# Decode attention with a gated MLP on one core: all eight sets inside PE's loop, and the last weight rows as 512-column products

## The chip, the cores and the metric

The kernel runs on one core of a Trainium2 chip. The time is device time in microseconds for one execution; several executions are timed and their median is given. One execution is also recorded by the hardware profiler, and all rows below come from that one. In them PE is the matrix engine (PEld its weight loads), DVE the vector engine, ACT the scalar engine, POOL GpSimd, SP the engine whose queue issues the large loads.

## What is computed

Four sequences, one new token each. From `x` (4 x 512):

```python
x = A_x
g = _sigmoid((x * gate_w).sum(-1, keepdims=True))
a = _A_ref(x, A_k_cache, A_v_cache, A_wq, A_wo)   # 32 query heads, 8 kv heads, head size 128, last 4096 cached rows
b = _B_ref(x, B_W_gate, B_W_up, B_W_down)         # relu(x Wg) * (x Wu), then times Wd; inner width 1792
return g * a + (1 - g) * b
```

`a` is `softmax(q k^T / sqrt(128)) v` over the window, with four query heads to a kv head, then times `wo` (4096 x 512). The caches are bf16, and the window of both is 67 MB, out of 81 MB that the kernel loads. The output is 4 x 512.

## The kernel before

**Sets.** The work on the caches is cut into eight sets. A set is one sequence and four kv heads: K of a set is 4 MB (`Ksb[:, s % 2]`), V is 4 MB (`Vsb[:, s % 2]`), both double buffered. For a set s PE turns K over in 16 fills of four transposes each (`kt(s, i)`, L363, four PSUM banks `TR` in turn); ACT copies 11 of the fills back over K (L368) and DVE five (L370). After every four fills `scores(s, bank)` multiplies with the queries `qS` (eight products of 512 columns in four column groups of 32, L384, banks `SCB[0]` and `SCB[1]` in turn), and DVE masks the result into `sc` with a running maximum (L392). One set later follow, for s - 1: `maximum` (DVE over the banks' maxima, a PE product that spreads it, DVE to `negmax`; L398 to L403), `exponent` on ACT in two pieces (L411), `turn` on DVE (transposes to `pT`, L418), `values` on PE (64 products with V in four column groups into bank `OB`, L429) and a copy to `osb` (L435). Two sets later `combine` sums the groups on PE (L443, L447) and DVE scales into `oq` (L450, L451).

**Order.** Every engine has a list of operations, written out by hand in one order for all engines; `Program.need` turns each operation's waits (named events) into semaphore counts. PE alone runs part of its list as a loop: `turn_edge` marks places in the list, and `emit` checks that the turns between the marks have the same waits and emits one of them in a hardware loop, lowering the semaphores at the end of a turn by what a turn raises (L138 to L145). PE's list is: the queries and the gate; set 0's fills and scores by themselves; set 1; then three turns of two sets each (2 and 3, 4 and 5, 6 and 7); then the end. Where PE waits for an event that DVE counts on its other semaphore, `need` takes the next event on the semaphore that PE reads.

**Loads.** All large loads are in SP's queue, in this order: Wq (to `Wbig`), K0, K1, V0, K2, V1, K3, V2, and so on to K7, V6, then Wg, Wu, V7, Wd, and `wo` in five pieces (rows 0 to 15, 16 to 25, 26 to 29 of 32, and rows 30 and 31 in two halves; `WO_CUTS`). K of set s waits for `("SC", s - 2, 3)`, the last scores of the set that held its buffer; V of set s waits for `("PV", s - 2, 3)`, the last values product there; both from set 2 on. Wd waits for `("PV", 6, 3)`, and `wo`, which takes Wq's place in `Wbig`, for the query products. Each load runs on 16 DMA engines, and its semaphore is raised by each of them when its sixteenth is in place: 16 landing marks to a load.

**Start.** POOL makes identity, mask and selection matrices and clears `xw`, `xT` and `qW` (L252 to L284). `x` and `gate_w` come by ACT's queue. DVE spreads x (`XW`, L290), PE transposes it, DVE copies it to `gwB` and `xT` (L298, L301), PE and ACT make the gate; PE multiplies with Wq (32 products of 512 columns in four column groups, L314), ACT casts (L324), PE transposes the heads (L332), DVE and ACT each write half of `qW` (L338), POOL copies a set's part to `qS` (L343).

**End.** After the loop: `maximum`, `exponent` and `turn` of set 7, `combine(6)`, `gateup` (Wg and Wu, L459), values of set 7 when V7 has landed, `combine(7)`, then the two output products. They add up in one bank, `AB = SCB[0]`, four column groups of 128 output columns each: for each of Wd's 14 rows of 128 and `wo`'s 32, four products of 128 columns (`product`, L530), so 56 and 128 of them. `wo`'s wait piece by piece for their load. DVE and ACT then copy two groups each (L548, L550) and SP stores.

Of the kernel before, what the change touches and what calls it, by code (L numbers as in the profile page):

```python
# [19 lines left out]
NSET = 8  # L20
# [6 lines left out]
NTR = 4  # L27
# [4 lines left out]
WO_CUTS = (0, 16, 26, 30)  # L32
ACT_TAKES = (0, 1, 4, 6, 8, 9, 11, 12, 13, 14, 15)
LOOP_FIRST = 2
LOOP_TURNS = 3


class Program:

# [8 lines left out]
    def __init__(self):  # L48
        self.ops = {e: [] for e in self.ENGINES}
        self.events = {}  # L50
        self.counts = {}
        self.history = {}
        self.dmas = []
        self.turns = []
        self.shared = {}

    def op(self, engine, fn, name=None, waits=(), sem=None):
        if name is not None:
            assert name not in self.events, name
            sem = sem or engine  # L60
            self.counts[sem] = self.counts.get(sem, 0) + 1
            self.events[name] = (sem, self.counts[sem], engine, len(self.ops[engine]))
            self.history.setdefault(sem, []).append(len(self.ops[engine]))
        self.ops[engine].append((fn, name, tuple(waits), False))

# [12 lines left out]
    def need(self, engine, waits):  # L78
        need = {}
        for w in waits:  # L80
            if w is None:
                continue
            s, n, by, at = self.events[w]
            for own, mine in (("dve", "vd"), ("act", "va")):
                want = mine if engine == "pe" else own
                if by == own and s in (own, mine) and s != want:
                    s = want
                    n = 1 + sum(1 for k in self.history[s] if k < at)
                    assert n <= self.counts[s], w
            need[s] = max(need.get(s, 0), n)  # L90
        return need
# [5 lines left out]
    def emit_list(self, eng, sems, engine, ops, shift, seen):  # L97
        for fn, name, waits, is_dma in ops:
# [5 lines left out]
            if fn is None:  # L104
                continue
# [17 lines left out]
    def emit(self, engine, eng, sems):  # L123
# [6 lines left out]
        first = self.signature(ops[t[0]:t[1]], {})  # L130
        for k in range(1, len(t) - 1):
            shift = {s: k * n for s, n in self.lowered.items() if s not in self.shared}
            assert self.signature(ops[t[k]:t[k + 1]], shift) == first, k
        with eng.Fori(0, len(t) - 1):
            self.emit_list(eng, sems, engine, ops[t[0]:t[1]], {}, {})
# [3 lines left out]
        shift = {s: (len(t) - 1) * n for s, n in self.lowered.items() if s not in self.shared}  # L139
        self.emit_list(eng, sems, engine, ops[t[-1]:], shift, {})  # L140


def bass_gated_mix__sliding_block_cached__glu_gated_reglu__decode_kernel(
# [13 lines left out]
    with ExitStack() as ctx:  # L157
# [7 lines left out]
        pT = sb("pT", [128, 2, 2048], BF16)  # L165
# [11 lines left out]
        xT = sb("xT", [128, 4, 32], BF16)  # L177
        xw = sb("xw", [5, 512], FP32)
        gwB = sb("gwB", [128, 512], BF16)
        gsb = sb("gsb", [128, 8], FP32)  # L180
        qW = sb("qW", [128, NSET, 2, 32], BF16)
        qS = sb("qS", [128, 2, 2, 32], BF16)
        mx = sb("mx", [128, 2, NBANK], FP32)
        mcol = sb("mcol", [128, 2], FP32)
# [3 lines left out]
        rowsum = sb("rowsum", [128, 2, NPIECE], FP32)  # L188
        osb = sb("osb", [128, 2, 256], FP32)
# [5 lines left out]
        hT = sb("hT", [128, NFT * 4], BF16)  # L195
        outr = sb("outr", [4, 512], BF16)
        banks = [ctx.enter_context(nc.psum_tensor("bank%d" % i, [128, 512], FP32)) for i in range(8)]
# [9 lines left out]
        Wq3 = Wbig[:, :].rearrange("p (t w) -> p t w", t=4)  # L207
# [4 lines left out]
        def loop_sem(kind, s):  # L212
            if kind == "K" and s >= LOOP_FIRST or kind == "V" and LOOP_FIRST - 1 <= s < NSET - 1:
                return "%s%d" % (kind, s % 2)
            return None
# [9 lines left out]
        def load_v(s):  # L225
            P.dma("sp", lambda e: e.dma_start(Vsb[:, s % 2, :], heads(A_v_cache, s)), ("V", s),
                  [("PV", s - 2, 3)] if s >= 2 else [], sem=loop_sem("V", s))
# [15 lines left out]
        for k in range(len(WO_CUTS) - 1):  # L243
            lo, hi = 512 * WO_CUTS[k], 512 * WO_CUTS[k + 1]
            P.dma("sp", lambda e, lo=lo, hi=hi: e.dma_start(Wbig[:, lo:hi], wo_src[:, lo:hi]), ("WO", k), [("Q",)])
        wo_src3 = A_wo.rearrange("(p i) w -> p i w", p=128)
        for u in range(2):
            P.dma("sp", lambda e, u=u: e.dma_start(Wo3[:, WO_CUTS[-1]:32, 256 * u:256 * u + 256],
                                                   wo_src3[:, WO_CUTS[-1]:32, 256 * u:256 * u + 256]), ("WOL", u), [("Q",)])
# [8 lines left out]
        P.op("pool", lambda e: e.memset(xw[:, :], 0.0), ("XW0",))  # L258
        P.op("pool", lambda e: e.memset(xT[:, :, :].rearrange("p t r -> p (t r)"), 0.0))
        P.op("pool", lambda e: e.memset(qW[:, :, :, :].rearrange("p s h w -> p (s h w)"), 0.0), ("QZ",))  # L260
# [34 lines left out]
        for t in range(4):  # L295
            P.op("pe", lambda e, t=t: e.transpose(FB[:, t * 8:t * 8 + 5], xv[0:5, t, :], identw[0:5, 0:5]),  # L296
                 ("XT",) if t == 3 else None, [("XW",), ("IDENTW",)])
        P.op("dve", lambda e: e.tensor_copy(gwB[:, :].rearrange("p (t m) -> p t m", t=4),  # L298
                                            fx[:, :, 4:5].to_broadcast([128, 4, 128])),
             None, [("XT",)])  # L300
        P.op("dve", lambda e: e.tensor_copy(xT[:, :, 0:4], fx[:, :, 0:4]), ("XTC",), [("XT",), ("QZ",)], sem="vd")  # L301
        for t in range(4):
            P.op("pe", lambda e, t=t: e.matmul(FB[:, 32:36], gwB[:, t * 128:(t + 1) * 128], xT[:, t, 0:4],
                                               start=(t == 0), stop=(t == 3)),
                 ("Z",) if t == 3 else None, [("XTC",)])
# [31 lines left out]
        for cc in range(2):  # L337
            P.op(("dve", "act")[cc], lambda e, cc=cc: (e.copy if cc else e.tensor_copy)(  # L338
                qW[64 * cc:64 * cc + 64, :, :, 16 * cc:16 * cc + 16].rearrange("p s o j -> p (s o) j"),
                FB[64 * cc:64 * cc + 64, 64:320].rearrange("p (k j) -> p k j", j=16)),  # L340
                ("QC", cc), [("QT",), ("QZ",)])
# [5 lines left out]
        fills = []  # L347

        def copy_done(f):
            return ("KTC",) + fills[f]  # L350

        def kt(s, i):
            f = len(fills)
            fills.append((s, i))
            bk = TR[f % NTR]
            for cc in range(4):
                c = 4 * i + cc
                w = []
                if cc == 0:
                    w = [("K", s), ("IDENTW",)] + ([copy_done(f - NTR)] if f >= NTR else [])  # L360
                    if i == NTR - 1 and s >= 1:
                        w.append(("NEGMAX", s - 1))
# [9 lines left out]
        def scores(s, bank):  # L372
# [4 lines left out]
            for o in range(2):  # L377
                for a in range(4):
                    w = []
                    if a == 0 and o == 0:  # L380
                        w = [("KTC", s, 4 * bank + u) for u in range(4)] + [("QS", s)]
                        if prev >= 0:
                            w.append(("SCC", prev // NBANK, prev % NBANK))
# [12 lines left out]
        def maximum(s):  # L396
            par = s % 2
            P.op("dve", lambda e: e.tensor_reduce(mcol[:, par:par + 1], mx[:, par, :], AXIS.X, ALU.max),  # L398
                 ("MCOL", s), [("SCC", s, NBANK - 1), ("MT", s - 2) if s >= 2 else None], sem="vd")
            P.op("pe", lambda e: e.matmul(TR[NTR - 1][:, 0:128], mcol[:, par:par + 1].to_broadcast([128, 128]), identw[:, :],  # L400
                                          start=True, stop=True),
                 ("MT", s), [("MCOL", s), ("KTC", s, NFILL - 1)])
            P.op("dve", lambda e: e.tensor_tensor_reduce(  # L403
                mrow[:, :], TR[NTR - 1][:, 0:128], qmask[:, :], -SCALE, -LOWEST, ALU.add, ALU.min, negmax[:, par:par + 1]),
# [4 lines left out]
        def exponent(s, k):  # L409
            par = s % 2  # L410
            P.op("act", lambda e: e.activation(  # L411
                sc[:, par, k * PW:(k + 1) * PW], sc[:, par, k * PW:(k + 1) * PW], ACTF.Exp,
                bias=negmax[:, par:par + 1], scale=SCALE, accum_out=rowsum[:, par, k:k + 1]),
                ("EXP", s, k), [("NEGMAX", s), ("SUMS", s - 2) if s >= 2 else None])

        def turn(s, k):
            par = s % 2
            P.op("dve", lambda e: e.transpose(pT[:, par, k * PW:(k + 1) * PW], sc[:, par, k * PW:(k + 1) * PW]),  # L418
                 ("PTT", s, k), [("EXP", s, k), ("PV", s - 2, 3) if s >= 2 else None], sem="vd")

        def values(s, k):
            par = s % 2
            for c in range(16):
                g = c % 4
                w = []
                if c == 0:
                    w = [("PTT", s, k * NPIECE // 4), ("V", s), ("OSB", s - 1) if s >= 1 else None]
# [6 lines left out]
            if k == 3:  # L434
                P.op("act", lambda e: e.copy(osb[:, par, :], OB[:, 0:256]), ("OSB", s),  # L435
                     [("PV", s, 3), ("SUMS", s - 2) if s >= 2 else None], sem="va")

        def combine(s):
            par, b, half = s % 2, s // 2, s % 2
            r = slice(64 * half, 64 * half + 64)  # L440
            for k in range(8):
# [3 lines left out]
                     [("OSB", s), ("WSUM",), ("OQ", s - 1) if s >= 1 else None])  # L445
            for k in range(NPIECE):
                P.op("pe", lambda e, k=k: e.matmul(FB[r, 416:417], Wsum[:, :], rowsum[:, par, k:k + 1],  # L447
                                                   start=(k == 0), stop=(k == NPIECE - 1)),
                     ("SUMS", s) if k == NPIECE - 1 else None, [])
            P.op("dve", lambda e: e.reciprocal(recip[r, par:par + 1], FB[r, 416:417]), ("RECIP", s), [("SUMS", s)])  # L450
# [4 lines left out]
        def gateup():  # L455
            for which, W, key in ((0, Wg, "WG"), (1, Wu, "WU")):
                for t in range(4):
                    for g in range(4):
# [4 lines left out]
                            [(key,)] + [copy_done(f) for f in range(NSET * NFILL - NTR, NSET * NFILL)])  # L463
# [7 lines left out]
                hT[:, :].rearrange("p (i b) -> p i b", b=4),  # L471
# [5 lines left out]
        for i in range(NFILL):  # L477
            kt(0, i)
            if i % 4 == 3 and i > 3:
                scores(0, i // 4 - 1)  # L480
        scores(0, 3)
        for s in range(1, NSET):
            if s >= LOOP_FIRST and (s - LOOP_FIRST) % 2 == 0:
# [12 lines left out]
            if s >= 2:  # L496
                combine(s - 2)
# [35 lines left out]
        for i in range(NFT):  # L533
            for cb in range(4):
                product(hT[:, 4 * i:4 * i + 4], Wd[:, i, :], cb, i == 0, False, None,
                        [("WD",), ("H",), ("SCC", NSET - 1, NBANK - 1)])
        for k in range(len(WO_CUTS) - 1):
            for i in range(WO_CUTS[k], WO_CUTS[k + 1]):
                for cb in range(4):
                    product(oq3[:, :, i], Wo3[:, i, :], cb, False, False, None, [("WO", k), ("OQ", NSET - 1)])  # L540
# [12 lines left out]
        per = {}  # L553
        for s in ("vd", "va"):
            eng = {"vd": "dve", "va": "act"}[s]
            a = P.events[("KTC", LOOP_FIRST, next(i for i in range(NFILL) if (i in ACT_TAKES) == (s == "va")))][1]
            b = P.events[("KTC", LOOP_FIRST + 2, next(i for i in range(NFILL) if (i in ACT_TAKES) == (s == "va")))][1]
            per[s] = b - a
        per["pq"] = 2
# [3 lines left out]
        P.lowered = per  # L563

# [3 lines left out]
        nc.sync.dma_start(Wbig[:, :], A_wq.rearrange("(p t) w -> p (t w)", p=128)).then_inc(sems["wq"], 16)  # L568
# [51 lines left out]
```

## Time and profile before

| | us |
|---|---|
| median of three runs | 196.4 (196.17 to 196.47) |
| the profiled execution | 196.17 |
| its span, first to last instruction | 194.9 |
| PE, DVE, ACT, POOL busy | 139.4, 77.2, 76.1, 9.5 |
| mean granted PE clock | 0.889 |
| K and V, issue to landing, median | 21.8 and 30.9 |

The span is cut into 40 slices in the page's second part; a digit is the busy share of a slice in tenths. The clock is the share of full speed that PE was granted; in this trace it is 1.0 or 0.5. The chain of waits starts at the last instruction and goes back, at each step to what released it. In a group row, "line engine operation out<-in" is followed by shapes, count, busy time, mean duration and the idle time before it. In the timeline a row is start, duration, engine, line, operation, count.

### The profile page before, as it was taken

The page shows a single profiled execution, that of the slowest core. Times are in us where ns is not written, and L with a number is a line of the kernel's source. Part 1 is how long each engine was busy: PE and PEld are TensorE (multiplying, and loading weights), DVE is VectorE, ACT ScalarE, POOL GpSimd, SP SyncE. Part 2 cuts the span into 40 slices and gives each one's busy share as a digit, 9 for nine tenths or more (in the row PEclk, how much of TensorE's full clock was granted, in tenths as well). Part 3 has the DMA queues.
Part 4 walks back from the last instruction along what each step waited for, and adds up shares of the span by engine and source line. Part 5 has one row for each costly group of instructions (what it writes and reads, how often), then busy time and mean ns, then how long its engine had stood idle before and what let it go on. Part 6 is the DMA issues. An engine that isn't in the chain of part 4 may idle for free.

```text
span 194.9 us, 3931 instructions
## 1 busy us (share of the span) xinstructions
PE 139.4 (72%) x1728; PEld 103.6 (53%) x1728; DVE 77.2 (40%) x169; ACT 76.1 (39%) x140; POOL 9.5 (5%) x41
## 2 busy tenths in 40 slices
PE   0135399688789818996898189995995899643834
PEld 0112397366468517763685177854773777422633
DVE  0100045477268302762583026623952456280101
ACT  2005136494285404462854043445641545240001
POOL 8700000000000000000000000000000000000000
PEclk9999999999999995899999855799999579995855
DMA  6999999999999999999999999999999999998993
GB/s 216 444 437 430 430 444 434 430 430 430 440 430 417 437 427 430 437 437 427 430 430 444 430 437 430 430 430 430 430 430 430 430 386 427 479 430 381 429 397 102
DMA packets 3884, 81.16 MB, mean 416 GB/s; under 512 B 409, under 2 KB 930, under 8 KB 1058
## 3 DMA queue, kind: packets, MB, share of 16 engines
q1 hardware_dynamic: 3864, 81.01, 97.3%
q8 instruction: 8, 0.13, 0.3%
q14 instruction: 2, 0.02, 0.0%
q10 hardware_dynamic: 10, 0.01, 0.0%
HBM read 81.01 MB, written 0.00 MB: 416 GB/s over the span
## 4 chain that ended last, share of the span: by engine, by line
DMA 55%; PE 36%; ACT 4%; DVE 3%; issue 1%; SPq 1%; DVEq 0%
DMA Ksb<-in_A_k_cache_dram 43%; PE bank L363 23%; DMA Wbig<-in_A_wo_dram 11%; PE bank L384 6%; ACT Ksb L368 3%; PE bank L429 2%; PE bank L443 2%; DVE Ksb L370 1%; PE bank L530 1%; ACT L411 1%; ACT sc L411 1%; DVE pT L418 1%; PE bank L447 0%; DVE sc L392 0%; PE bank L400 0%
## 5 line engine op out<-in xcount | busy, mean ns | idle before, releaser
L363 PE MATMUL bank<-identw,Ksb 128*128 128x128 f32 x512 | 77.0, 307 | 20.8 <-DMA Ksb<-in_A_k_cache_dram 14.9
L363 PEld LDWEIGHTS bank<-identw,Ksb 128*128 128x128 f32 x512 | 65.3, 158 | 31.6 <-DMA Ksb<-in_A_k_cache_dram 15.8
L368 ACT COPY Ksb<-bank 128x512 f32<-128x512 f32 x88 | 48.7, 589 | 73.0 <-PE bank L363 73.0
L370 DVE COPY Ksb<-bank 128x512 f32<-128x512 f32 x40 | 27.3, 684 | 40.6 <-PE bank L363 40.6
L392 DVE CUSTOM_DVE_ANT_0 sc<-bank,mask 128x512 bf16<-128x512 f32 x32 | 21.8, 682 | 28.8 <-PE bank L384 28.8
L429 PE MATMUL bank<-Vsb,pT 128*32 128x256 bf16 x512 | 20.9, 291 | 6.1 <-DMA Vsb<-in_A_v_cache_dram 6.1
L384 PE MATMUL bank<-Ksb,qS 128*32 128x512 bf16 x256 | 21.0, 405 | 1.8 <-ACT Ksb L368 0.9
L418 DVE STREAM_TRANSPOSE pT<-sc 128x1024 bf16<-128x1024 bf16 x16 | 19.7, 1236 | 2.1 <-ACT sc L411 2.0
L429 PEld LDWEIGHTS bank<-Vsb,pT 128*32 128x32 bf16 x512 | 13.3, 101 | 12.6 <-issue 8.8
L411 ACT ACTIVATE sc<-sc,negmax 128x1024 bf16<-128x1024 bf16 x16 | 18.4, 1151 | 1.9 <-DVE negmax L403 1.8
L443 PEld LDWEIGHTS bank<-osb,Wsel 128*64 128x64 f32 x128 | 9.4, 157 | 4.8 <-issue 3.7
L443 PE MATMUL bank<-osb,Wsel 128*64 128x32 f32 x128 | 10.3, 239 | 0.5 <-ACT osb L435 0.5
L435 ACT COPY osb<-bank 128x256 f32<-128x256 f32 x8 | 3.0, 373 | 17.6 <-PE bank L429 17.6
L400 PE MATMUL bank<-identw,mcol 128*128 128x128 f32 x16 | 3.8, 320 | 7.8 <-DVE mcol L398 4.7
L384 PEld LDWEIGHTS bank<-Ksb,qS 128*32 128x32 bf16 x256 | 4.1, 95 | 9.0 <-ACT Ksb L368 5.7
L400 PEld LDWEIGHTS bank<-identw,mcol 128*128 128x128 f32 x16 | 2.4, 187 | 10.2 <-DVE mcol L398 8.4
L343 POOL COPY qS<-qW 128x64 bf16<-128x64 bf16 x8 | 1.8, 238 | 120.5 <-PE bank L384 110.8
L530 PE MATMUL bank<-Wbig,oq 128*4 128x128 bf16 x128 | 4.2, 307 | 3.8 <-DMA Wbig<-in_A_wo_dram 3.8
L296 PE MATMUL bank<-identw,xw 5*128 5x5 f32 x4 | 0.6, 263 | 8.6 <-DVE xw L290 8.6
L450 DVE RECIPROCAL recip<-bank 64x1 f32<-64x1 f32 x8 | 1.3, 159 | 11.4 <-PE bank L447 11.4
L530 PEld LDWEIGHTS bank<-Wbig,oq 128*4 128x4 bf16 x128 | 3.1, 118 | 4.8 <-DMA Wbig<-in_A_wo_dram 4.7
L314 PE MATMUL bank<-Wbig,xT 128*32 128x512 bf16 x32 | 3.6, 631 | 2.7 <-DMA Wbig<-in_A_wq_dram 2.7
(55 smaller groups left out, 45.4 us busy)
## 6 DMA issues: line engine op xcount, KB each, us to landing
Ksb<-in_A_k_cache_dram SPq DMA_DIRECT2D x8, 4096.0 KB, 21.8
Vsb<-in_A_v_cache_dram SPq DMA_DIRECT2D x8, 4096.0 KB, 30.9
Wbig<-in_A_wq_dram SPq DMA_DIRECT2D x1, 4096.0 KB, 12.2
Wbig<-in_A_wo_dram SPq DMA_DIRECT2D x1, 2048.0 KB, 19.5
Ksb<-in_B_W_gate_dram SPq DMA_DIRECT2D x1, 1792.0 KB, 17.1
Ksb<-in_B_W_up_dram SPq DMA_DIRECT2D x1, 1792.0 KB, 21.0
Vsb<-in_B_W_down_dram SPq DMA_DIRECT2D x1, 1792.0 KB, 15.0
Wbig<-in_A_wo_dram SPq DMA_DIRECT2D x1, 1280.0 KB, 22.1
```

What stands on the lines that cost most here:

```text
L314: P.op("pe", lambda e, half=half, t=t, g=g, col=col: e.matmul(SCB[half][32 * g:32 * g + 32, 0:512], xT[:, t, :], Wq3[:, t, col:col + 512], ...
L363: P.op("pe", lambda e, bk=bk, cc=cc, c=c, s=s: e.transpose(bk[:, cc * 128:(cc + 1) * 128], Kw[:, s % 2, c * 128:(c + 1) * 128], identw[:, :]),
L368: P.op("act", lambda e: e.copy(dst, bk[:, :]), ("KTC", s, i), [("KT", s, i)], sem="va")
L370: P.op("dve", lambda e: e.tensor_copy(dst, bk[:, :]), ("KTC", s, i), [("KT", s, i)], sem="vd")
L384: P.op("pe", lambda e, a=a, o=o: e.matmul(bk[32 * a:32 * a + 32, 0:512], qS[:, s % 2, o, :], k4[:, 16 * bank:16 * bank + 16, 32 * a:32 * a ...
L392: P.op("dve", lambda e: e.tensor_tensor_reduce(sc[:, s % 2, bank * 512:(bank + 1) * 512], bk[:, :], mask[:, :], 1.0, LOWEST, ALU.add, ALU.max,
L400: P.op("pe", lambda e: e.matmul(TR[NTR - 1][:, 0:128], mcol[:, par:par + 1].to_broadcast([128, 128]), identw[:, :], start=True, stop=True) ...
L411: P.op("act", lambda e: e.activation(sc[:, par, k * PW:(k + 1) * PW], sc[:, par, k * PW:(k + 1) * PW], ACTF.Exp, bias=negmax[:, par:par + ...
L418: P.op("dve", lambda e: e.transpose(pT[:, par, k * PW:(k + 1) * PW], sc[:, par, k * PW:(k + 1) * PW]), ("PTT", s, k), [("EXP", s, k), ("PV ...
L429: P.op("pe", lambda e, c=c, g=g, blk=blk: e.matmul(OB[32 * g:32 * g + 32, 0:256], pT[:, par, 32 * blk:32 * blk + 32], Vsb[:, par, 256 * bl ...
L443: P.op("pe", lambda e, k=k, lo=lo: e.matmul(FB[r, 384:416], Wsel[:, lo:lo + 64], osb[:, par, 32 * k:32 * k + 32], start=(k == 0), stop=(k ...
L530: P.op("pe", lambda e: e.matmul(AB[32 * cb:32 * cb + 4, 0:128], stat, mov[:, 128 * cb:128 * cb + 128], start=start, stop=stop, tile_positi ...
```

## The change

**PE's loop.** All eight sets run in four turns of two. The prologue's own copy of sets 0 and 1 is gone. In the first turn the work that belongs to sets before the first is real on PE and empty elsewhere: `maximum(-1)`, `values(-1, k)`, `combine(-2)` and `combine(-1)` issue their PE products (on zeroed `pT`, `osb`, `rowsum`, `mcol`, and on whatever lies in `Vsb[:, 1]`, which is Wq), while DVE and ACT only raise the semaphores that the real operations would have raised, with a one-element memset or copy (`signal`, `blank`). Ahead of the loop PE raises three semaphores by one turn's worth (`ahead`), so that waits on the turn before the first are met.

**What follows from it.** Wq is loaded to `Vsb[:, 1]` instead of `Wbig`, and V1 therefore waits for `("PV", -1, 3)`; V0 waits for nothing as before. `wo` no longer waits for the query products. The buffers that must start as zeros lie in one tensor `zs` (with `xw`, `xT`, `qW`, `hT`), cleared by one POOL memset of 2,600 f32 columns in place of three. `gwB`, `xT` and both halves of `qW` are copied by ACT. The spread maximum goes to `SCB[0]` instead of a `TR` bank; the wait for `negmax` moves from the fourth fill to the first scores.

**The end.** Wd's 14 rows and `wo`'s rows 0 to 25 are no longer four products of 128 columns each. Each row is one product of 512 columns; 40 rows go to four column groups of the bank `DB = SCB[1]` in turn (row n to group n % 4). ACT copies the bank to `bulk` (128 x 512 f32). Rows 26 to 29 go to `AB` as before. Then four f32 products of `S32` with `bulk` add the four groups into `AB`, and rows 30 and 31 follow as before.

```diff
+    def signal(self, engine, name, sem):
+        self.op(engine, SIGNAL, name, (), sem)
...
+            ahead = w not in self.events
+            if ahead:
+                if engine != "pe":
+                    continue
+                w = (w[0], w[1] + 2) + tuple(w[2:])
...
+            if fn is SIGNAL:
+                sem = self.events[name][0]
+                signals += 1
+                if at + 1 == len(ops) or ops[at + 1][0] is not SIGNAL or self.events[ops[at + 1][1]][0] != sem:
+                    self.blanks += 1
+                    self.blank[engine](eng, self.blanks).then_inc(sems[sem], signals)
+                    signals = 0
                 continue
...
+        for s, n in self.ahead.items():
+            eng.sem_inc(sems[s], n)
         with eng.Fori(0, len(t) - 1):
-            self.emit_list(eng, sems, engine, ops[t[0]:t[1]], {}, {})
+            self.emit_list(eng, sems, engine, ops[t[0]:t[1]], shift(0), {})
             eng.drain()
             for s, n in self.lowered.items():
                 eng.sem_inc(sems[s], -n)
...
-        Wq3 = Wbig[:, :].rearrange("p (t w) -> p t w", t=4)
+        Wq3 = Vsb[:, 1, :].rearrange("p (t w) -> p t w", t=4)
...
             P.dma("sp", lambda e: e.dma_start(Vsb[:, s % 2, :], heads(A_v_cache, s)), ("V", s),
-                  [("PV", s - 2, 3)] if s >= 2 else [], sem=loop_sem("V", s))
+                  [("PV", s - 2, 3)] if s >= 1 else [], sem=loop_sem("V", s))
...
-        P.op("pool", lambda e: e.memset(xw[:, :], 0.0), ("XW0",))
-        P.op("pool", lambda e: e.memset(xT[:, :, :].rearrange("p t r -> p (t r)"), 0.0))
-        P.op("pool", lambda e: e.memset(qW[:, :, :, :].rearrange("p s h w -> p (s h w)"), 0.0), ("QZ",))
+        P.op("pool", lambda e: e.memset(zs[:, 1024:], 0.0), ("XW0",))
...
-                    if i == NTR - 1 and s >= 1:
-                        w.append(("NEGMAX", s - 1))
...
+                        if bank == 0:
+                            w.append(("NEGMAX", s - 1))
...
-            P.op("pe", lambda e: e.matmul(TR[NTR - 1][:, 0:128], mcol[:, par:par + 1].to_broadcast([128, 128]), identw[:, :],
+            P.op("pe", lambda e: e.matmul(SCB[0][:, 0:128], mcol[:, par:par + 1].to_broadcast([128, 128]), identw[:, :],
                                           start=True, stop=True),
-                 ("MT", s), [("MCOL", s), ("KTC", s, NFILL - 1)])
+                 ("MT", s), [("MCOL", s)])
+            if s < 0:
+                P.signal("dve", ("NEGMAX", s), "dve")
+                return
...
-        for i in range(NFILL):
-            kt(0, i)
-            if i % 4 == 3 and i > 3:
-                scores(0, i // 4 - 1)
-        scores(0, 3)
-        for s in range(1, NSET):
-            if s >= LOOP_FIRST and (s - LOOP_FIRST) % 2 == 0:
+        P.events[("V", -1)] = ("V1", 16, None, 0)
+        for s in range(NSET):
+            if s % 2 == 0:
                 P.turn_edge()
...
-            if s >= 2:
-                combine(s - 2)
+            combine(s - 2)
...
-        for i in range(NFT):
-            for cb in range(4):
-                product(hT[:, 4 * i:4 * i + 4], Wd[:, i, :], cb, i == 0, False, None,
-                        [("WD",), ("H",), ("SCC", NSET - 1, NBANK - 1)])
-        for k in range(len(WO_CUTS) - 1):
+        DB = SCB[1]
+        rows = [(hT[:, i, :] if i < 4 else hT[:, i, 0:4], Wd[:, i, :], [("WD",), ("H",), ("SCC", NSET - 1, NBANK - 1)])
+                for i in range(NFT)]
+        for k in range(BULK_PIECES):
+            rows += [(oq3[:, :, i], Wo3[:, i, :], [("WO", k), ("OQ", NSET - 1)]) for i in range(WO_CUTS[k], WO_CUTS[k + 1])]
+        for n, (stat, mov, waits) in enumerate(rows):
+            g = n % 4
+            P.op("pe", lambda e, g=g, n=n, stat=stat, mov=mov: e.matmul(
+                DB[32 * g:32 * g + (32 if n < 4 else 4), 0:512], stat, mov, start=(n < 4), stop=(n >= len(rows) - 4),
+                tile_position=(0, 32 * g)), ("BULK",) if n == len(rows) - 1 else None, waits)
+        P.op("act", lambda e: e.copy(bulk[:, :], DB[:, :]), ("BULKC",), [("BULK",)], sem="va")
+        for k in range(BULK_PIECES, len(WO_CUTS) - 1):
             for i in range(WO_CUTS[k], WO_CUTS[k + 1]):
                 for cb in range(4):
-                    product(oq3[:, :, i], Wo3[:, i, :], cb, False, False, None, [("WO", k), ("OQ", NSET - 1)])
+                    product(oq3[:, :, i], Wo3[:, i, :], cb, i == WO_CUTS[BULK_PIECES], False, None,
+                            [("WO", k), ("OQ", NSET - 1), ("NEGMAX", NSET - 1)])
+        for cb in range(4):
+            product(S32[:, 0:4], bulk, cb, False, False, None, [("BULKC",), ("WSUM",)])
```

## The prediction

> **What bounds the kernel now.** I read the page's row of busy DMA engines first, then the chain of waits, then the timeline and the table of windows at the end.
>
> ```profile
> DMA  6999999999999999999999999999999999998993
> ...
> q1 hardware_dynamic: 3864, 81.01, 97.3%
> q8 instruction: 8, 0.13, 0.3%
> ```
>
> Forty columns are forty slices of the span: between the first and the last the 16 DMA engines are full. Loading 81 MB sets the time; PE (72% busy), DVE and ACT run beside it. So a part of the change moves the time only if it moves the start of the loading, lets it run dry, moves the landing of the last piece, or changes what is left after that. The chain shows the last:
>
> ```profile
> 168.71 22.15 DMA Wbig<-in_A_wo_dram
> 190.86 0.04 issue
> 190.91 2.05 PE bank L530 x60
> 192.96 0.02 issue
> 192.98 0.28 DVE outr L548
> 193.26 0.32 DVEq L569
> ```
>
> At 190.86 wo's second piece (rows 16 to 25) is complete. By the trace's landing marks rows 26 to 29 follow at 192.09, rows 30 and 31 in two halves at 192.43 and 192.78. PE works each off as it lands, so little is exposed: the last product starts at 192.89 and takes 0.31 (193.20), the second copies end at 193.58, the output is issued at 193.61, the span ends at 194.93. This execution took 196.17 (1.24 around the span); the median shown is 196.4, 0.23 more.
>
> ```profile
> 191.00:192.00 1.00, 1.00 (x40) 0.86 (x36) 0.00 (x0) 0.00 (x0) 0.00 (x0) 0.50 0.57 183
> ...
> 13.04 3.61 PE L314 MATMUL bank<-Wbig,xT 128*32 128x512 bf16 x32 [2.70 <-DMA Wbig<-in_A_wq_dram]
> ```
>
> The window row (PE, its loads, DVE, ACT, POOL, then the clock) says that PE runs at half clock (0.50) in the tail. The second line is the nearest row to the new products: 512 columns in four groups, eight rounds of four, started 0.427 apart, each product 0.634 long. 0.427 for 512 columns is the tail's rate too: there 128 columns take 0.107 a round.
>
> **The tail (decides).** Before, the ten rows that land at 190.86 are 40 products in ten rounds: 10 x 0.107 = 1.07, ending before the next piece lands. After, they are ten products of 512 columns, numbers 30 to 39, so groups 2,3,0,1,2,3,0,1,2,3: three rounds. The streamed time is the same per column, so nothing is won: last start 190.91 + 2 x 0.427 = 191.76, end + 0.634 = 192.40. Only now can ACT copy the bank (128x512 f32: 0.589, the row of L368) from 192.43 to 193.02. Then four f32 products fold the four groups into the accumulator. Each f32 product is two passes (L400: 16 for eight calls). A pass over 128 columns at half clock costs 0.213 (L363 at half clock starts every 0.213; L400's 275 ns at full clock is 56 more than the 219 of a bf16 product of 128 columns, which puts f32 at two cycles a column). Two passes of one call lie in one group and follow each other; the next call's first pass can start beside the second. In program order the starts are 193.06, +0.213, +0.427, +0.640, and the last pass +0.853. Behind these in PE's queue stand the eight products of rows 30 and 31, whose data has landed: the last starts at about +1.17 and ends +1.48, at 194.54. Before: 193.20. **Tail: +1.34.** Lower bound: if the four groups' passes run side by side, 2 x 0.213 + 0.107 + 0.31 = 0.84 after 193.06, 193.90, +0.70. Rows 26 to 29 (16 products, 0.43 + 0.31) are done while ACT copies. I take +1.2, nearer the upper end, because every row of products in the trace starts in program order.
> The Trainium skill, TensorEngine Tiling (Array Packing), section Key Properties, says that tiles work independently and that different tiles can load and multiply in parallel; by that the tail is the +0.70. No run of before has f32 products in several groups.
>
> The work ahead of it has cover: Wd's rows (56 products, 1.20, at 184.00) become 14 (four rounds, 1.1 or 1.9 at half clock), with 2.6 idle before rows 0 to 15 land at 187.73; those become 16 products, 4 x 0.427 + 0.2 = 1.9 against 1.88, done at 189.7, 1.2 ahead of 190.86.
>
> **Code packets (small gain, -0.1).** The trace's packet list has eight packets of 16,384 bytes on queue 8, of 1.00 to 1.17 us, at 31.7, 51.0, 59.9, 69.5, 89.9, 182.3, 188.7 and 192.4, and a pair of 8,192 at 60.7 and 61.0. Each sits on one DMA engine, and that engine stays late. K's first load reaches its 16 landing marks within 0.49; wo's second piece within 2.06: seven engines in 0.33, nine (as many as packets by then) 1.27 to 2.06 late. The last engine decides, so these packets cost up to 2.06 - 0.49 = 1.57. Queue 8 is PE's: by 31.7 PE had done 236 loads and products, the packets stop in the repeated turns, and eight packets for some 2,000 loads and products of code are one per 250. After, the code is 112 ahead of the loop, 728 in it (two sets of 182 pairs), about 420 behind it (maximum 4, combines 80, gate and up 64, values 128, bulk 80, the rest 64): 1,260, five packets, three of them in the first turn. But fewer late engines do not make the latest one earlier: a lag of 1.73 to 1.86 is there after the very first packet, 2.02 after those at 60. I take -0.1; bounds 0 and -0.3, or the full -1.57 if none hit (a rival).
>
> **The first turn (hidden, if K2 is issued in time).** The turn's first set now carries maximum(-1), combine(-2) and values(-1) on PE. SP queues K2 behind SC(0,3), then V1 behind PV(-1,3), which was free; behind those stand K3 and all other loads. Queued ahead are Wq, K0, K1, V0, whose first engine is free at 41.62. The first load's packets started 1.03 to 1.71 after its issue, so K2 must be issued by about 40.2; before it was
>
> ```profile
> 35.68 0.53 SPq L222 DMA_DIRECT2D Ksb<-in_A_k_cache_dram  x1
> ```
>
> After: K0 lands at 22.68 as before. Six fills 5.1 (0.855 apart until 28.6), scores 0.8, combine 1.3 (1.26 or 2.23 by the chain's rows at full and half clock), four fills 1.9, scores 0.6, four fills 1.9, scores 0.6, then values 0.5, fill 0.6, values 0.55, fill 0.6, its copy 0.65, scores 0.65: 38.4. Margin 1.8. V1 follows by about 0.7, under K2's 9.7. Set 1 then runs from 39 to about 55 where it ended at 51.4; its K3 is issued about 55, with V1 loading until 62.8. By set 3, which waits for K3's landing at 72.82, nothing is left of it. The added last turn edge (a drain, some semaphore steps) and the blank signals (a one-element DVE memset or ACT copy each, on engines with idle time there) lie in the same margin.
>
> **Free edits.** The NEGMAX wait moves from the fourth fill to the scores. On PE it is counted by DVE's next event, the copy of fill 2 (the chain's 0.70 "DVE Ksb L370" at 75.64 and its like); that stall goes, but the next set still waits for its K: 0. POOL's one memset of 2,600 columns takes about 2.2 (0.8 ns a column between the 128- and 512-column rows, plus 0.1) for three of 1.1 elapsed: POOL ends at 10.2 instead of 9.1, hidden because XW waits for gate_w's landing at 7.94 and mask and Wsum are needed after 28. If POOL's rate were five times slower, XW would be late and Wq's product with it; even then there are 4 idle us before K0. gwB and xT on ACT: 0.6 + 0.2 against 0.69 + 0.16, 2.9 ahead of Wq's landing. Both halves of qW on ACT: +0.4, with 3.5 idle before K0. Wq's new place and wo's dropped wait leave SP's order as it was; wo is still behind Wd's wait.
>
> **Sum.** 196.17 + 1.2 - 0.1 = 197.3 for that execution; with the 0.23 to the median, **197.5**.
>
> **Rivals.**
> *Tail hidden.* PE is at full clock in the tail: rounds 0.216, bulk ends at 191.75, copy 192.38, the fold 4 x 0.107 + 0.22 until 193.03; rows 30 and 31 end at 193.2 as before. Total 196.2 to 196.8. For: PE had clock 1.00 from 182.2 to 185.6. Against: 0.50 in every window from 187 on, and the waits for wo stay.
> By the Trainium skill, TensorE: Matmul & The Clock Gate, Part 1, full clock needs a busy window of about 3.4 us; the trace agrees with half clock here, its longest busy stretches after 185 are 1.9 and 2.3.
> *Code packets decide (faster).* If PE's smaller code brings none of the 16 KB packets before wo's last piece, the last engine is up to 1.57 earlier: 196.4 + 1.2 - 1.57 = 196.0, and with the +0.70 tail 195.5. It decides from zero late engines (or if the late ones left are those that start early, lag 1.3 for 2.0). For: packets fall from eight to five and the lag is the largest thing at the end that can go. Against: three crossings lie in the first turn, and the 8 KB pair is on another queue.
> *K2 late (slower).* With PE at half clock through set 0, as in set 5 (111.72 to 131.15, 19.4, less the 0.7 stall), SC(0,3) is at 41.4: a hole of 1.2 in the loading, never regained: 198.7.
>
> **Chances.** Forecast (196.9 to 198.2) 0.62; tail hidden 0.15; code packets 0.13; K2 late 0.10. A measurement here can tell about 0.2%, 0.4 us. Faster (under 196.0): most of the packets' case, 0.12. Same: the hidden tail and the packets' rest, 0.16. Slower: 0.72. Range 195.9 to 198.7: the fastest of the packets' case and the worst of K2's lie outside.
>
> **What would show it.** Right: wo's second piece complete near 190.9 as before; after it an ACT copy of 0.59, then f32 products, the output issued near 194.9. First step wrong: the last product ends within 0.3 of 193.2. Packets: landing marks of the last piece within 1 us of each other. First turn wrong: K2 issued after 40.2 and a slice under 9 near 42. Wrong altogether if a stage waits for code at a turn's edge, or the last landing moves by over 0.5.

## The result and the profile after

The changed kernel takes 196.96 us (median of 7, 196.87 to 197.38) where before takes 196.25 (median of 7): a ratio of 1.0037, 95% interval 1.0025 to 1.0049, so 0.71 slower, where 1.1 was forecast (197.5 for the 196.4 then known). Ratios and their intervals leave out executions over 1.5% above the fastest of their kernel; there are two, both in experiment 4. The profiled execution after took 197.02, its span is 195.8; before it was 196.17 and 194.9.

Loading still fills the span. From the page after, the busy share of the DMA engines in 40 slices, and two of the queues (packets, MB, share of 16 engines' span):

```profile
DMA  6999999999999999999999999999999999999991
...
q1 hardware_dynamic: 3864, 81.01, 96.9%
q8 instruction: 5, 0.08, 0.2%
```

There are five packets of code on queue 8 in place of eight. No slice shows a hole, and the last one is emptier than before: what grew lies behind the loading. The end of the chain of waits after (start, duration, what):

```profile
166.63 24.19 DMA Wbig<-in_A_wo_dram
190.82 0.04 issue
190.87 1.47 PE bank L572 x8
192.33 0.02 issue
192.36 0.59 ACT bulk L575
192.95 0.04 issue
193.00 0.82 PE bank L562 x16
193.82 0.02 issue
193.84 0.28 DVE outr L590
194.12 0.32 DVEq L611
```

`wo`'s second piece lands at 190.82 (190.86 before), and the last landing mark of its last piece is at 192.81 (192.78). Before, one step of PE stood between these landings and the output copies. Now three steps stand there: ten products of 512 columns, the bank copy on ACT, then the fold (the f32 products that add the four groups) with rows 30 and 31. The clock was at half, as before. The window row after (busy time of PE, its loads, DVE, ACT and POOL, then the clock, the DMA share and GB/s):

```profile
191.00:192.00 1.00, 1.00 (x10) 0.13 (x2) 0.00 (x0) 0.00 (x0) 0.00 (x0) 0.50 0.38 124
```

The timeline of the end after, then SP's issue of K2:

```profile
192.99 0.11 PEld L562 LDWEIGHTS bank<-bulk,S 128*4 128x4 f32 x8 [0.54 <-ACT bulk L575]
193.00 0.61 PE L562 MATMUL bank<-bulk,S 128*4 128x128 f32 x8 [0.26 <-ACT bulk L575]
...
193.38 0.44 PE L562 MATMUL bank<-Wbig,oq 128*4 128x128 bf16 x8
193.84 0.54 ACT L592 CAST outr<-bank 4x128 bf16<-4x128 f32 x2 [0.90 <-PE bank L562]
...
194.47 0.35 SPq L616 DMA_DIRECT2D out_dram<-outr  x1
```

```profile
38.36 0.54 SPq L253 DMA_DIRECT2D Ksb<-in_A_k_cache_dram  x1
```

Before, the same end read:

```profile
190.91 2.30 PE L530 MATMUL bank<-Wbig,oq 128*4 128x128 bf16 x64 [1.25 <-DMA Wbig<-in_A_wo_dram]
...
192.98 0.54 ACT L550 CAST outr<-bank 4x128 bf16<-4x128 f32 x2 [10.29 <-PE bank L530]
192.98 0.60 DVE L548 CAST outr<-bank 4x128 bf16<-4x128 f32 x2 [8.35 <-PE bank L530]
193.61 0.35 SPq L574 DMA_DIRECT2D out_dram<-outr  x1
```

The output is issued 0.86 later (194.47 for 193.61). 0.62 of it is the end of the last product (193.82 for 193.20). The other 0.24 comes from the output copies. Before, the first copy of each engine began at 192.98, when half of the columns were done and PE still had the rest to do, so that little more than the second copy lay behind the last product. I call the copies staged for that. Now both halves are done within 0.02 of each other, and each engine makes its two copies one after the other behind the last product.

### The profile page after: what moved, and what is told of

It reads as the page before. It is cut to its first block, busy times and chain, and to the rows that moved or that the text cites. A ratio compares the mean times of both kernels' runs of the same rounds, so it can differ in the third digit from the quotient of the medians.

```text
span 195.8 us, 3935 instructions
## 1 busy us (share of the span) xinstructions
PE 142.7 (73%) x1722; PEld 106.5 (54%) x1722; DVE 75.8 (39%) x172; ACT 79.3 (41%) x146; POOL 10.6 (5%) x39
## 4 chain that ended last, share of the span: by engine, by line
DMA 57%; PE 37%; ACT 2%; DVE 1%; SPq 1%; issue 1%; DVEq 0%
DMA Ksb<-in_A_k_cache_dram 44%; PE bank L383 24%; DMA Wbig<-in_A_wo_dram 12%; PE bank L405 6%; PE bank L461 3%; PE bank L477 3%; ACT Ksb L388 2%; PE bank L572 1%; DVE Ksb L390 1%; PE bank L481 1%; PE bank L562 0%; DVE sc L413 0%; ACT bulk L575 0%; PE bank L424 0%; SPq L276 0%
## 5 line engine op out<-in xcount | busy, mean ns | idle before, releaser
L383 PEld LDWEIGHTS bank<-identw,Ksb 128*128 128x128 f32 x512 | 68.0, 162 | 22.7 <-DMA Ksb<-in_A_k_cache_dram 15.5
L461 PE MATMUL bank<-Vsb,zs 128*32 128x256 bf16 x576 | 22.9, 285 | 8.3 <-DMA Vsb<-in_A_v_cache_dram 8.3
L461 PEld LDWEIGHTS bank<-Vsb,zs 128*32 128x32 bf16 x576 | 14.6, 99 | 15.5 <-issue 11.4
L450 DVE STREAM_TRANSPOSE zs<-sc 128x1024 bf16<-128x1024 bf16 x16 | 19.7, 1237 | 3.0 <-ACT sc L440 2.8
L477 PEld LDWEIGHTS bank<-zs,Wsel 128*64 128x64 f32 x160 | 10.1, 138 | 4.8 <-issue 4.0
L477 PE MATMUL bank<-zs,Wsel 128*64 128x32 f32 x160 | 11.2, 224 | 0.5 <-ACT zs L469 0.5
L469 ACT COPY zs<-bank 128x256 f32<-128x256 f32 x8 | 3.0, 372 | 19.3 <-PE bank L461 19.3
L424 PE MATMUL bank<-identw,zs 128*128 128x128 f32 x18 | 4.3, 323 | 8.1 <-DVE zs L422 7.9
L572 PE MATMUL bank<-Wbig,oq 128*4 128x512 bf16 x26 | 3.0, 566 | 4.6 <-DMA Wbig<-in_A_wo_dram 4.6
L343 PE MATMUL bank<-Vsb,zs 128*32 128x512 bf16 x32 | 3.6, 631 | 3.1 <-DMA Vsb<-in_A_wq_dram 3.1
```

Source lines behind the costliest of these rows:

```text
L343: P.op("pe", lambda e, half=half, t=t, g=g, col=col: e.matmul(SCB[half][32 * g:32 * g + 32, 0:512], xT[:, t, :], Wq3[:, t, col:col + 512], ...
L383: P.op("pe", lambda e, bk=bk, cc=cc, c=c, s=s: e.transpose(bk[:, cc * 128:(cc + 1) * 128], Kw[:, s % 2, c * 128:(c + 1) * 128], identw[:, :]),
L424: P.op("pe", lambda e: e.matmul(SCB[0][:, 0:128], mcol[:, par:par + 1].to_broadcast([128, 128]), identw[:, :], start=True, stop=True), ("M ...
L461: P.op("pe", lambda e, c=c, g=g, blk=blk: e.matmul(OB[32 * g:32 * g + 32, 0:256], pT[:, par, 32 * blk:32 * blk + 32], Vsb[:, par, 256 * bl ...
L477: P.op("pe", lambda e, k=k, lo=lo: e.matmul(FB[r, 384:416], Wsel[:, lo:lo + 64], osb[:, par, 32 * k:32 * k + 32], start=(k == 0), stop=(k ...
L572: P.op("pe", lambda e, g=g, n=n, stat=stat, mov=mov: e.matmul(DB[32 * g:32 * g + (32 if n < 4 else 4), 0:512], stat, mov, start=(n < 4), s ...
```

## The experiments

Three theories were tested. **End**: all that was lost lies behind `wo`'s second piece. **Loop**: the empty sets of the first turn or the code cost it. **Clock**: the longer chain at the end is exposed only because PE runs it at half clock. Each run was timed beside before; a ratio is that of its time to before's.

**1. All but the end** (`e1`): the changed kernel with products of 128 columns for all rows, as before.

```diff
-        for n, (stat, mov, waits) in enumerate(rows):
...
-        P.op("act", lambda e: e.copy(bulk[:, :], DB[:, :]), ("BULKC",), [("BULK",)], sem="va")
...
+        for i in range(NFT):
+            for cb in range(4):
+                product(hT[:, i, 0:4], Wd[:, i, :], cb, i == 0, False, None,
+                        [("WD",), ("H",), ("SCC", NSET - 1, NBANK - 1), ("NEGMAX", NSET - 1)])
```

> All of the change but the end: eight sets in four turns, Wq in Vsb, the new copies; Wd and wo as products of 128 columns as before. Theory 'end' (what was lost lies wholly behind wo's second piece: bank copy, fold, and output copies that now start together): within 0.2 of before, 196.1 to 196.4, wo's last piece at 192.8, output issued at 193.6. Theory 'loop' (the empty sets, the first turn or the packets of code cost it): 196.8 to 197.1, with K2 issued late or the last landing later. Six packets of code of 16 KB by the count of one per 250 loads and products (1,260 + 224).

Measured: 196.22 (before beside it 196.24), ratio 1.0000, 0.9992 to 1.0009; six packets, last mark 192.81, output issued at 193.66. Within the 0.2 us of this interval, the loop, the moved Wq and the new copies together cost and gain nothing.

**2. The end alone** (`e2`): before, with the new end put in place of its own (and `hT` 32 wide, cleared by one more POOL memset).

```diff
-                product(hT[:, 4 * i:4 * i + 4], Wd[:, i, :], cb, i == 0, False, None,
...
+        for n, (stat, mov, waits) in enumerate(rows):
...
+        P.op("act", lambda e: e.copy(bulk[:, :], DB[:, :]), ("BULKC",), [("BULK",)], sem="va")
```

> Before's loop of three turns and its start, with the new end alone (40 products of 512 columns, bank copy, fold). Theory 'end': 196.9 to 197.1, output issued at about 194.45, last piece at 192.8. Theory 'loop': 196.1 to 196.4. Seven or eight packets of code.

Measured: 197.19, ratio 1.0043, 1.0030 to 1.0056; 0.09 above the range expected. In the profiled execution the last mark came at 192.94, 0.13 later than after. Its timeline has the same rows as after:

```profile
191.03 1.45 PE L544 MATMUL bank<-Wbig,oq 128*4 128x512 bf16 x10 [1.24 <-DMA Wbig<-in_A_wo_dram]
...
192.52 0.59 ACT L547 COPY bulk<-bank 128x512 f32<-128x512 f32 x1 [11.36 <-PE bank L544]
...
193.16 0.61 PE L534 MATMUL bank<-bulk,S 128*4 128x128 f32 x8 [0.25 <-ACT bulk L547]
...
194.63 0.35 SPq L588 DMA_DIRECT2D out_dram<-outr  x1
```

With experiment 1, the end makes the whole loss, and the theory "loop" falls.

**3. Fold early** (`e3`). Only rows that have landed well before the end go to the 512-column products:

```diff
-BULK_PIECES = 2
+BULK_PIECES = 1
...
+        for cb in range(4):
+            product(S32[:, 0:4], bulk, cb, True, False, None, [("BULKC",), ("WSUM",), ("NEGMAX", NSET - 1)])
         for k in range(BULK_PIECES, len(WO_CUTS) - 1):
```

> The changed kernel, but only Wd's rows and wo's rows 0 to 15 go to the 512-column products; their bank is copied and folded ahead of wo's second piece, whose rows are products of 128 columns as before. Theory 'end': rows 0 to 15 end at 189.5, the copy at 190.1, the fold at 190.8, all before 190.86; after that as before: 196.1 to 196.4. Rival 'form' (the 512-column products themselves are the slower form): stays at 196.7 or more.

Measured: 196.18, ratio 1.0002, 0.9993 to 1.0012. The bank copy and the fold are done before the second piece lands:

```profile
189.07 0.59 ACT L575 COPY bulk<-bank 128x512 f32<-128x512 f32 x1 [6.63 <-PE bank L572]
...
189.71 0.61 PE L562 MATMUL bank<-bulk,S 128*4 128x128 f32 x8 [0.69 <-ACT bulk L575]
...
190.90 2.29 PE L562 MATMUL bank<-Wbig,oq 128*4 128x128 bf16 x64 [0.59 <-DMA Wbig<-in_A_wo_dram]
```

For the 30 rows that keep the 512-column form, the form with its copy and fold costs nothing when it is done ahead of the second piece. Rows 16 to 25 went back to 128 columns here, so this run alone does not part their form from the place of the copy and the fold; experiment 5 keeps that form.

**4. Clock kept up with twenty products** (`e4`): the changed kernel with 10, 8 and 2 products more that nobody reads, to keep PE busy while it waits for `wo`.

```diff
+            if n == NFT:
+                filler(10)
+            if n == NFT + WO_CUTS[1]:
+                filler(8)
...
+        filler(2)
```

> The changed kernel with 20 products more that nobody reads (512 columns, into a free bank), 10 ahead of wo's rows 0 to 15, 8 ahead of its second piece, 2 behind it, so that PE's clock stays up to the end. If the half clock makes the loss: second piece 190.87 to 191.75 in place of 192.33, copy until 192.35, fold and last products until about 193.1: 196.1 to 196.3. If the order copy, fold, output copies makes it whatever the clock: 196.6 to 196.9. If the clock row stays at 0.5, it tells nothing.

Measured: 197.42 (eight executions, 196.03 to 199.05), ratio 1.0051, 1.0017 to 1.0085, an interval that also holds the changed kernel's 1.0037. In the profiled execution the clock came up at 187.55, but the added products stood in front of `wo`'s rows:

```profile
190.29 1.90 PE L563 MATMUL bank<-mask,ident 128*128 128x512 bf16 x8
...
192.12 0.82 PE L581 MATMUL bank<-Wbig,oq 128*4 128x512 bf16 x10
```

The second piece landed at 190.62 and was begun at 192.12. So the total says nothing about the clock; the ten products did take 0.82 in place of 1.45.

**5. Clock kept up with nine products** (`e4b`): the same with fewer of them.

```diff
+            if n == NFT:
+                filler(6)
+            if n == NFT + WO_CUTS[1]:
+                filler(3)
```

> As the run with 20 added products, but few enough not to stand in front of wo's pieces when PE is at half clock: 6 ahead of rows 0 to 15, 3 ahead of the second piece, none behind it (nobody reads them). Theory 'clock': where the clock is up at 190.9, rows 16 to 25 end at 191.8, the output is issued at 193.5 to 193.7 and the execution takes 196.0 to 196.3; where it is at half, 196.9 as before. So a median between 196.1 and 196.9 and more spread. Theory 'order' (copy, fold, output copies whatever the clock): no execution under 196.6.

Measured: 196.12 (11 executions, 195.95 to 196.96), ratio 0.9996, 0.9987 to 1.0005: 0.84 below the changed kernel. From the window table and the timeline:

```profile
191.00:192.00 1.00, 0.57 (x10) 0.07 (x2) 0.00 (x0) 0.39 (x1) 0.00 (x0) 1.00 0.32 103
```

```profile
190.75 0.82 PE L581 MATMUL bank<-Wbig,oq 128*4 128x512 bf16 x10 [1.30 <-DMA Wbig<-in_A_wo_dram]
191.61 0.59 ACT L584 COPY bulk<-bank 128x512 f32<-128x512 f32 x1 [9.03 <-PE bank L581]
...
192.25 0.40 PE L567 MATMUL bank<-bulk,S 128*4 128x128 f32 x8
...
193.41 0.35 SPq L625 DMA_DIRECT2D out_dram<-outr  x1
```

At full clock the fold is over by 192.65, before the last piece lands (192.70, 0.11 earlier than after): the chain is hidden, and the output copies are staged again, from 192.79 on. "Clock" and "end" are one story: 1.45 + 0.59 + 0.61 at half clock overrun the landing of the last piece, 0.82 + 0.59 + 0.40 at full clock do not. Between 191 and 192 the clock is 1.00 in all four profiled executions with this filling or one like it (experiments 5, 6, 7 and 9) and 0.50 in all six with none (before, after, experiments 1, 2, 3 and 8). The one execution at 196.96 may have had half clock; it was not profiled, so that is not shown.

**6. The same filling on before** (`e7`).

```diff
         for k in range(len(WO_CUTS) - 1):
+            filler((6, 3, 0)[k])
```

> Before with 6 and 3 added products that nobody reads, ahead of wo's rows 0 to 15 and of its second piece. By theory 'clock' full clock is worth little here, since PE waits for each piece: the last product ends 0.1 earlier (0.22 for 0.31) and the second output copies can start at once: 196.0 to 196.3. If PE's speed at the end counted fully: 195.6 or less.

Measured: 196.08, ratio 0.9994, 0.9985 to 1.0003.

```profile
192.74 0.61 ACT L556 CAST outr<-bank 4x128 bf16<-4x128 f32 x2 [10.11 <-PE bank L535]
...
193.41 0.35 SPq L580 DMA_DIRECT2D out_dram<-outr  x1
```

The output is issued at 193.41 (193.61 without the filling), but the interval holds 1: no gain over before is shown. At full clock the old and the new end are level (196.08, 196.12).

**7. Early fold with the filling** (`e8`): the edit of 3, and

```diff
+            if n == NFT:
+                filler(6)
...
+        filler(3)
         P.op("act", lambda e: e.copy(bulk[:, :], DB[:, :]), ("BULKC",), [("BULK",)], sem="va")
```

> The kernel with the early fold, with 6 and 3 added products that nobody reads: ahead of rows 0 to 15, and behind them while ACT copies. Theory 'end': 195.9 to 196.3, no slower than before and at best 0.2 faster. If the added products delay the fold behind wo's second piece, 196.4 to 196.9.

Measured: 196.03, ratio 0.9992, 0.9983 to 1.0001. This is the lowest median of several executions, 0.93 below the changed kernel, but its interval holds 1: it is not shown to beat before.

**8. No loop at all** (`e5`): before, with PE's list written out.

```diff
-            if kind == "K" and s >= LOOP_FIRST or kind == "V" and LOOP_FIRST - 1 <= s < NSET - 1:
-                return "%s%d" % (kind, s % 2)
             return None
...
-        if engine != "pe":
+        if True:
             self.emit_list(eng, sems, engine, ops, {}, {})
```

> Before's work with PE's list written out, no loop: some 3,440 loads and products, so 13 or 14 packets of code of 16 KB and the pair of 8 KB, in place of eight and the pair. Theory 'latest engine' (a packet makes its DMA engine late, only the latest engine counts, each is hit once): nearly all 16 engines late, the last landing mark of wo's last piece still at 192.6 to 193.1, time 196.0 to 196.5. Rival 'packets add up' (or one engine is hit twice): that mark 1 us or more later, time 197.0 to 198.0; then fewer packets than before should have gained, and the loop is worth something.

Measured: 197.58, ratio 1.0074, 1.0061 to 1.0088. From its page:

```profile
q8 instruction: 13, 0.21, 0.4%
```

and the lag of a load, which is how far its latest landing mark stands behind its first, by the trace's marks:

```
                        before   after   no loop
first load (Wq)          0.52     0.63     0.88
V1                       2.02     1.96     2.07
V5 (from 138.8)          2.03     2.01     2.23
K7 (from 148.5)          2.04     2.01     3.18
wo's last piece          1.97     1.85     3.14
its last mark at       192.78   192.81   194.15
```

When V5 landed, eight packets of 16 KB and the pair of 8 KB had come, and ten of its marks were late (1.6 to 2.23), six were not (0 to 0.4). Behind the next packet, at 141.2, the latest mark jumps by 0.95 (to 3.18 at K7), while the first marks of loads still come 9.7 apart. At the end four marks stand at 3.0 to 3.1, and still six are within 0.31. The marks do not name their engines, but their counts say that packets come upon the same engines again; the expectation that each of 13 would find its own fell. The last mark comes 1.37 later (194.15 for 192.78), and that is the whole loss of 1.33.

**9. Which engines** (`e9`), one execution: the kernel of `e8` with four tiny loads more behind `wo`'s last piece, of 8, 4, 2 and 1 rows. Besides one mark at its issue, each gave as many landing marks as it has rows.

```diff
+        for n, k in enumerate((8, 4, 2, 1)):
+            P.dma("sp", lambda e, n=n, k=k: e.dma_start(pr[0:k, n, :], A_wo[512:512 + k, 0:256]), ("PR", n))
```

> The kernel with the early fold and the short filling, and behind wo's last piece four loads of 8, 4, 2 and 1 rows of 512 bytes that nobody reads, to see by their landing marks which DMA engines are late. Theory 'latest engine': the marks fall on the same steps as those of wo's last piece (0 to 0.5, and 0.9 to 2.0 later), and the nested sets of engines say which ones stand where. If all marks lie together, the lag is not an engine's but a load's, and the theory of late engines falls. Time 195.9 to 196.6.

Measured: 195.94. The load of one row lands at 191.73 and that of two at 191.54 and 192.11: its second mark is 0.57 behind the first. Of the eight marks of the first load four lie within 0.17 and the others 0.58, 0.84, 1.45 and 1.55 after its first. These are the steps of `wo`'s last piece (ten marks within 0.30, then 0.58, 0.84, 1.43 to 1.68), which speaks for a lag of the engine and not of the load. If a load of eight rows uses half of the engines, four of that half are late, so such loads would not keep the last piece clear of late engines; nothing built on that was tried.

## Why the prediction was right, and where its terms were off

**The bound, the landing, the first turn** held. The last mark moved by 0.03. K2 was issued at 38.36 (38.4 forecast), so the hole that the K2 rival asked for could not open; V1 followed at 38.94, K3 at 53.69 (55 forecast). Experiment 1 shows that all of it costs nothing.

**The tail** was right as a mechanism and too large: 1.2 was taken, 0.86 measured. The ten products ended at 192.33 (192.40 forecast), and the copy took 0.59 as forecast. The step that failed is the fold. It was reckoned "in program order", each call's first pass no earlier than the second pass of the call before it, with 1.48 to the end of the last product. By the trace's single records the four calls' first passes begin within 0.02 of each other at 193.00 and the four second ones at 193.16 to 193.18, so all four groups work side by side. From 193.00 to the end of the last product it is 0.82, where the forecast's lower bound had 0.84. The rows in four column groups that the forecast leaned on had one pass a call, so they could not speak to this.
The Trainium skill, TensorEngine Tiling (Array Packing), Key Properties, says that tiles work in parallel; here the trace agrees, 0.61 for eight passes that one after the other would take at least 8 x 0.213.
Against that, 0.24 was left out: before, the two halves of the last piece staged the output copies, and the fold in front of both halves undid that. So the last product ended 0.62 later, which is less than the lower bound of +0.70, and the total of 0.86 lies between the forecast's +0.70 and +1.34 only because of the 0.24 that the forecast had left out. That much was luck. The output was issued at 194.47, not near 194.9.

**The sum.** Of the 0.54 between 197.5 and 196.96, 0.25 lies in these terms: 197.27 stood for the profiled execution, 197.02 was measured (tail 0.34 less, the gain of 0.1 from the code missing). The other 0.29 lies in the step to the median: 0.23 was added, from a median of three, while the changed kernel's median is 0.06 below its profiled execution. Before's median of seven is 196.25.

**Code packets.** There were five, as counted, and the gain of 0.1 was 0. The faster rival fell: with four packets of 16 KB in place of seven by the time `wo`'s second piece landed, its lag was 2.03 (2.06 before), and the last piece's was 1.85, not within the 1 us that the rival asked for. What raises the lag further is a second packet on the same engine; experiment 8 shows that step, and before's loop already avoids it.
The Trainium skill, Runtime: NRT & Kernel Launch, Instruction fetch mechanics, calls the cost of crossing a 16 KiB boundary "mostly hidden". For PE's own work the trace agrees: without the loop, PE has no idle time over 0.1 within 3 us of the packets at 31.7, 60.9, 100.2 and 141.2. For a kernel that loading fills it does not: 1.37 at the last mark for five packets more.

**The hidden-tail rival** named the right condition: at full clock 196.12 was measured for its 196.2 to 196.8. It got 0.15 because before's clock was at half from 185.6 on; after's was at half from 188.1 on. Nothing in the change kept the clock up; the filling of experiment 5 did.

**Free edits.** POOL's memset took 2.27 (2.2 forecast), the copies to `gwB` and `xT` 0.59 and 0.18 (0.6 and 0.2). One thing was not foreseen: ACT loaded a table once more than before (1.28, at 9.77), between those copies and the gate; Wq landed at 13.2, so it was hidden.

A kernel without any packet of code before the end was not tried, so what the whole lag is worth stays an estimate.

## What to carry to other kernels

Where loading sets the time, count what moves the last landing and what comes behind it. Keep every step that works on early rows (here the bank copy and the fold) ahead of the last landing; fewer and longer products ahead of it gained nothing here. Price PE's work at the end at the clock that it will have there, and see what a step in front of two staged halves does to the staging. Packets of code made single DMA engines late here (by 1.27 to 2.06 in before's second piece of `wo`). More packets on other engines hardly moved the latest mark (2.03 with four of 16 KB, 2.06 with seven); a second one on the same engine moved it by 0.95.

## What the runs showed that was not expected

Six added products of 512 columns ahead of `wo`'s first piece and three between its first two kept the clock at 1.00 to the end (0.50 without) and took 0.84 off the changed kernel. Twenty took the clock up too, but stood in front of `wo`'s rows in PE's queue, and no gain was shown (196.03 to 199.05). f32 products of four column groups ran their passes side by side: eight of 128 columns in 0.61 at half clock, 0.40 at full.
